# Batch 0's first x made transposed and centred by TensorE, w1 and w2 loaded in other parts, and chunk 0 reordered

## The chip, the core and the metric

The kernel runs on one core of one Trainium2 chip. A core has five engines with an instruction stream each: TensorE (PE in the profile; PEld is its weight load), VectorE (DVE), ScalarE (ACT), GpSimd (POOL) and SyncE (SP). TensorE reads SBUF and writes PSUM, which has eight banks of 512 fp32 columns; the other engines bring results back. The metric is the device time of one execution in microseconds. The time before is 265.41 us, the median of three runs (265.18 to 265.62).

## The reference

Two layers in a row over 8 batches, 8 heads, 576 positions and 64 features a head: a linear attention without a position-by-position matrix, and a normalized two-layer network with a residual.

```
q_s = softmax(q, over features);  k_s = softmax(k, over positions)
kv  = einsum('bhsd,bhse->bhde', k_s, v)          # 64 x 64 per head
x   = einsum('bhsd,bhde->bhse', q_s, kv)         # heads side by side: 512 columns
xn  = (x - mean(x)) / sqrt(var(x) + 1e-6) * g
out = x + relu(xn @ w1) @ w2                     # w1 512 x 2048, w2 2048 x 512
```

All inputs and the output are fp32; the kernel computes its products in bf16. The factor 1/sqrt(var) belongs to a row, so it passes through the relu and both products, and the kernel applies it at the very end.

## The kernel before

The first 512 positions of each batch are one chunk of four tiles of 128 rows (chunks 0 to 7); the last 64 positions of all batches together are chunk 8. A chunk's work is: exp of q and k (ScalarE), the kv products with their division by the sums of exp(k), the transposed exp(q) ("eqT"), x = eqT times kv ("po" in PSUM, evicted to x), xn = 512 x minus the row sum, its transpose "xnT" with 512 columns per tile, then the first product with w1 (PSUM tiles "ph", relu to "hT") and the second with w2 ("pc"). From chunk 2 on, and in chunk 1's second product, a seven-product scheme is used; the change leaves it alone, apart from the last product of the last chunk.

The order of the work on each engine is the order in which the program issues it. `run(main, side)` writes it: `main` is a list of TensorE steps with weights, `side` a list of functions with a position, and a function is issued before the first main step whose summed weight has reached its position. A weight of 1 is a product of 512 moving columns. In chunk 0 the first product fills positions 0 to 64 and the second 64 to 128; in chunk 1 the first product over tiles 0, 1 (32 products of 256 columns, weight 0.5) fills positions 0 to 16, and tiles 2, 3 follow at 16.

What stands around the change:

- `first_batch` (L888) issues the loads and batch 0's start. Loads on SP: q of tiles 0, 1 and k by head pair. Loads on POOL, in order: v, q of tiles 2, 3, w1 in column parts (two of 256, three of 512), w2 in row parts of 512; `load_behind` adds batch 1's and 2's inputs.
- `warm` (L789) issues filler products on TensorE that nothing reads. `z0_mm` (L268) sums exp(k), `kv0_mm` (L284) makes kv of a head pair in PSUM, two pairs to a bank, and evicts them on VectorE.
- `po_half` (L391) makes half of x of tile 0 or 1 and evicts it on ScalarE with its row sum; `sum_halves`, `xn_out` and four transposes with L984 give xnT of tile 0. `exp_qt` is exp of one q tile, `eq_pT` (L877) and `xn_pT` (L880) are four transposes on TensorE and one copy on the engine named in the call; for chunk 0 `xn_pT` multiplies by `g_col` (L866), for the others it is a plain copy (L862 on ScalarE, L864 on VectorE).
- `q0_rest` (L991) is the row sums of exp(q) and x of a later tile of chunk 0, `x_fast` (L380) scales x and makes xn on VectorE, `square_sum` (L365) is ScalarE's sum of squares.
- `mm1_part` (L443) is one step of the first product over part of the tiles, `mm2_stream` (L493) one of the second, `y_out` (L464) the output.
- `mlp_steps` (L745) lists a chunk's main steps; the side lists are at L1044 for chunk 0 and in `second_side` (L818) for chunk 1.
- `last_products` (L574) is the last chunk's second product with its outputs and stores.

PSUM is handed out from two pools: six banks `mm_ps` and two `att_ps`; a tile waits until the bank's earlier user has been read.

Of the kernel before, what the change touches and what calls it, by code (L numbers as in the profile page):

```python
# [20 lines left out]
def kernel(  # L21
# [22 lines left out]
    T = 4  # L44
# [29 lines left out]
    scrap = const.tile([P, 512], BF16)  # L74
    bones = const.tile([P, 2], BF16)
    w1_sb = wts.tile([P, KO1, DH], BF16, tag="w1", name="w1_raw")
    w1g = const.tile([P, KO1, DH], BF16)
    g_col = const.tile([P, KO1], FP32)
    ident_f = const.tile([KO1, KO1], FP32)
# [14 lines left out]
    def load_w2(g4):  # L94
        rows = slice(4 * g4, 4 * g4 + 4)
        nc.gpsimd.dma_start(w2_sb[:, rows, :], w2_src[:, rows, :])
# [182 lines left out]
    def recip_z():  # L279

        kvbox["rz"] = sml.tile([P, NP], FP32, tag="rzk", name="rzk")
        nc.vector.reciprocal(kvbox["rz"], kvbox["z0"][:, 0:NP])

    def kv0_mm(j):  # L284

        if j % 2 == 0:
            kvbox["p0"] = att_ps.tile([P, 2, 256], FP32, tag="a", name="pkv")
        pkv = kvbox["p0"]
        for t in range(T0):
            for ps in halves:  # L290
                nc.tensor.matmul(
                    pkv[ps, j % 2, 0:D], eks[0][ps, j, t], raws["v0"][ps, j, t],
                    start=(t == 0), stop=(t == T0 - 1),
                )
        if j % 2:
            for ps in halves:
                nc.vector.tensor_mul(
                    kv_sb[ps, 0, j - 1 : j + 1, ps], pkv[ps, :, 0:D],
                    kvbox["rz"][ps, j - 1 : j + 1].to_broadcast([64, 2, D]),
                )  # L300

# [44 lines left out]
    def po_mm(c, t, i):  # L346


        if i == 0:
            pool, tag = (mm_ps, "m") if c == 0 and t >= 2 else (att_ps, "a")  # L350
            pobox["p"] = pobox[c, t] = pool.tile([P, DM], FP32, tag=tag, name="po")
# [39 lines left out]
    def po_half(t, half):  # L391

        pool, tag = (mm_ps, "m") if half else (att_ps, "a")
        po = pool.tile([P, DM], FP32, tag=tag, name="po")
        for i in range(2):
            j = 2 * half + i
            nc.tensor.matmul(
                po[:, i * P : i * P + P], eqTs[0][:, t, j, :], kv_sb[:, 0, j, :],
                start=True, stop=True,
            )  # L400
        x, st, _, _ = xs[0]
        nc.scalar.activation(
            x[:, t, DH2 * half : DH2 * half + DH2], po[:, 0:DH2], AF.Copy,
            accum_out=st[:, t, half : half + 1],
        )

    def sum_halves(t):
        _, st, _, mv = xs[0]
        nc.vector.tensor_add(mv[:, t, 0:1], st[:, t, 0:1], st[:, t, 1:2])
# [120 lines left out]
    def prod(n, bank, t, k, first=False, own=False):  # L530
# [13 lines left out]
        nc.tensor.matmul(hbox[bank][:, t], lhsT, rhs, start=first and (own or t == 0) and k == 0,  # L544
# [29 lines left out]
    def last_products(product):  # L574
# [6 lines left out]

        def stt(t, col, src, add=None):
# [17 lines left out]
        def own_bank():  # L600
            bank("d")

        def seed_e():
# [15 lines left out]
        product(4, "d", ts=(1,), own=True, at={  # L619
            15: [lambda: stt(3, 0, hbox["d"][:, 1], part(3, 0)), lambda: store(3, 1, 0)]})  # L620

    def mm2_fast(c):
# [3 lines left out]
        def product(n, name, first=False, at=None, ts=range(2), own=False, cut=None):  # L626
# [4 lines left out]
            for i, (t, k) in enumerate(order):  # L631

                def go(t=t, k=k, i=i):
                    if i == 0 and first:
                        bank(name)
                    prod(n, name, t, k, first or own, own)
# [3 lines left out]
                steps.append((0.5, go))  # L640
# [103 lines left out]

    def mlp_steps(c):  # L745
# [4 lines left out]
        if c == 0:  # L750
            full = range(0)
            parts = ((0, 2, 0, 1), (0, 2, 1, 1), (2, 2, 0, 1), (2, 2, 1, 1), (4, 4, 0, 2), (0, 4, 2, 1),
                     (0, 4, 3, 1), (4, 4, 2, 2), (8, 4, 0, 2), (8, 4, 2, 2), (12, 4, 0, 2), (12, 4, 2, 2))
        else:
            full, parts = range(8, KO2), ((0, 8, 0, 2), (0, 8, 2, 2))
        for m0, mn, t0, tn in parts:
# [5 lines left out]
        if c == 0:  # L762
            return first + [
                (1, lambda t=t, ko=ko: mm2_stream(c, t, ko))
                for n in range(4) for t in range(T) for ko in range(4 * n, 4 * n + 4)
# [52 lines left out]
    def second_side():  # L818

        s = [(p, lambda i=i: quarter_w2(i, 1)) for i, p in enumerate((8.5, 13, 44, 46))]  # L820
        s += [(8.0, lambda: xn_pT(1, 3, nc.vector))]
# [3 lines left out]
        s += [(9 + 2 * j, lambda j=j: cast_v(2, j)) for j in range(2)]  # L825
# [57 lines left out]
    def g_columns():  # L883
        gcp = mm_ps.tile([P, KO1], FP32, tag="m", name="gcp")
        nc.tensor.matmul(gcp, raws["g"], ident_f, start=True, stop=True)
        nc.vector.tensor_scalar_mul(out=g_col, in0=gcp, scalar1=1.0 / DM)

    def first_batch():  # L888
# [30 lines left out]
        nc.vector.memset(ones, 1.0)  # L919
        nc.vector.memset(bones, 0.0)  # L920
# [14 lines left out]
        load_w1(0, 256)  # L935
        load_w1(256, 256)
        for nb in range(1, 4):
            load_w1(512 * nb)
        load_w2(0)
        load_w2(1)  # L940
# [3 lines left out]
        warm(31)  # L944
        for t in range(2):
            exp_qt(0, t)
        exp_k0(0)
        exp_k0(1)
        norm_q(0, 0)
        norm_q(0, 1)  # L950
        eq_pT(0, 0, nc.scalar)
        g_columns()
        exp_k0(2)
        warm(5)
        z0_mm(0)
        z0_mm(1)
        exp_k0(3)
        eq_pT(0, 1, nc.vector)
        z0_mm(2)
        warm(3)  # L960
        z0_mm(3)
        recip_z()
        for j in range(NP):
            kv0_mm(j)
        warm(2)
        po_half(0, 0)
        warm(3)
        po_half(0, 1)
        po_half(1, 0)
        po_half(1, 1)  # L970
# [153 lines left out]
```

## Time and profile before

| | us |
|---|---|
| median of three runs | 265.41 |
| the profiled execution's own time | 265.6 |
| its span, first to last instruction | 263.6 |
| TensorE busy | 257.4 |
| VectorE busy | 217.4 |
| ScalarE busy | 178.8 |
| GpSimd busy | 76.0 |
| first product of chunk 0's first stage (L451) | 15.24 |
| first product of chunk 0's second stage (L497) | 31.84 |
| first product of chunk 1 (L451 on w1g) | 49.21 |

The times in the lower half are starts from the span's first instruction. The profile's views used below are these. The page's first part gives busy time by engine. The waits name the engine and line that waited, what it waited for, the total, how many times and the longest. The chain lists, in order of time, the work that ended last at each moment: start, length, what. A timeline gives start, length, engine, line, operation, written tile <- read tiles, shape and count. Windows give busy time, the share of the DMA engines and what they moved in a stretch. The granted TensorE clock was 0.999 of full speed.

### The profile page before, as it was taken

To read this page: it belongs to the slowest core of one execution; us is meant where nothing else is said; L and a number is where in the kernel's file an instruction comes from. 1 tells how busy PE (TensorE), PEld (TensorE's weight loads), DVE (VectorE), ACT (ScalarE), POOL (GpSimd) and SP (SyncE) were. 2 spreads that over 40 slices of the span, in tenths; PEclk is the share of its full clock that TensorE was granted. 3 is DMA by queue.
4 is the path that set the end of the run, shared out by engine and by line. 5 is a ranking of instruction groups with operands and counts; after the bars stand their busy time and mean duration, and the time that the engine had idled before them with its cause. 6 is when DMAs were issued, how large, how long until landed. Compare 5 with 4: busy or idle time off the path is not lost.

```text
span 263.6 us, 6818 instructions
## 1 busy us (share of the span) xinstructions
PE 257.4 (98%) x2708; PEld 218.1 (83%) x2711; DVE 217.4 (82%) x475; ACT 178.8 (68%) x350; POOL 76.0 (29%) x126
## 2 busy tenths in 40 slices
PE   8989999999999999999999999999999999999993
PEld 5778855775988998899889988998899888888882
DVE  4667797968989997989798979997999889877873
ACT  4467852896966888688868886788678377438400
POOL 8652316203049007600760076008200300030000
PEclk9999999999999999999999999999999999999999
DMA  6999999997986995799879957997804620521014
GB/s 219 256 204 208 338 208 315 271 155 233 207 151 197 325 136 97 197 308 155 93 215 298 139 99 237 297 135 146 256 6 79 161 82 12 71 90 72 0 42 119
DMA packets 69847, 45.00 MB, mean 171 GB/s; under 512 B 41460, under 2 KB 66040, under 8 KB 69816
## 3 DMA queue, kind: packets, MB, share of 16 engines
q1 hardware_dynamic: 48896, 21.76, 39.3%
q0 software_dynamic: 20320, 22.29, 38.9%
q10 hardware_dynamic: 600, 0.53, 0.6%
q8 instruction: 21, 0.34, 0.6%
q14 instruction: 10, 0.08, 0.1%
HBM read 36.70 MB, written 9.44 MB: 175 GB/s over the span
## 4 chain that ended last, share of the span: by engine, by line
PE 92%; DMA 4%; POOL 2%; issue 0%; ACT 0%; DVE 0%; POOLq 0%
PE ba L544 21%; PE bx L688 19%; PE bb L688 9%; PE ph L451 8%; PE bb L544 5%; PE be L544 5%; PE bc L544 5%; PE pc L497 5%; PE bc L688 5%; DMA w_raw<-in_moe_w_ch_dram 4%; PE ph L436 3%; PE po L353 3%; PE pkv L316 2%; PE ptr L860 1%; POOL v L931 1%; PE po L360 1%
## 5 line engine op out<-in xcount | busy, mean ns | idle before, releaser
L544 PEld LDWEIGHTS <-hs 128*128 128x128 bf16 x512 | 49.5, 98 | 5.7
L688 PEld LDWEIGHTS <-w_q 128*128 128x128 bf16 x448 | 43.1, 98 | 5.2 <-issue 0.2
L544 PEld LDWEIGHTS <-hT 128*128 128x128 bf16 x384 | 37.2, 98 | 4.4
L240 POOL TENSOR_TENSOR tq<-xnT 128x256 bf16<-128x256 bf16 x20 | 12.9, 661 | 78.6 <-DMA xnT<-xn 47.2
L688 PEld LDWEIGHTS <-w1g 128*128 128x128 bf16 x336 | 32.2, 98 | 3.9
L544 PE MATMUL ba<-w_q,hs 128*128 128x256 bf16 x256 | 31.7, 273 | 0.0
L688 PE MATMUL bx<-tq,w_q 128*128 128x256 bf16 x224 | 29.0, 273 | 0.0
L561 POOL DMA_DIRECT2D out_dram<-ot x28 | 15.3, 557 | 46.4 <-DVE ot L555 46.4
L367 ACT ACTIVATE scrap<-x,mv 128x512 bf16<-128x512 bf16 x36 | 25.9, 719 | 1.7 <-DVE x L383 1.3
L383 DVE SCALAR_TENSOR_TENSOR x<-po,rq 128x512 bf16<-128x512 f32 x34 | 23.3, 685 | 1.2 <-PE po L353 1.1
L712 ACT COPY bc<-bx 128x512 f32<-128x512 f32 x28 | 15.2, 594 | 13.0 <-PE bx L688 13.0
L719 DVE TENSOR_TENSOR bb<-bx,s 128x512 f32<-128x512 f32 x28 | 18.2, 694 | 6.3 <-ACT s L716 6.3
L730 ACT ACTIVATE hT<-bc 128x512 bf16<-128x512 f32 x28 | 15.3, 595 | 11.9 <-PE bc L688 11.9
L202 DVE TENSOR_REDUCE zq<-eq 128x16 f32<-128x1024 bf16 (+1 forms) x20 | 20.6, 1049 | 2.3 <-ACT eq L193 2.3
L528 DVE TENSOR_TENSOR hs<-hT 128x1024 bf16<-128x1024 bf16 x32 | 20.9, 674 | 0.9 <-ACT hT L730 0.5
L730 ACT ACTIVATE hT<-bb 128x512 bf16<-128x512 f32 x28 | 15.2, 595 | 8.8 <-PE bb L688 8.8
L353 PE MATMUL po<-kv_sb,eqT 128*128 128x128 bf16 x120 | 20.5, 219 | 0.0
L722 DVE TENSOR_TENSOR hT<-bx,s 128x512 bf16<-128x512 f32 x28 | 18.0, 684 | 3.0 <-PE bx L688 3.0
L569 ACT COPY s<-ba 128x512 f32<-128x512 f32 x15 | 8.7, 579 | 12.5 <-PE ba L544 7.8
L544 PE MATMUL ba<-w_sb,hT 128*128 128x256 bf16 x128 | 16.7, 273 | 0.0
L544 PE MATMUL bb<-w_q,hs 128*128 128x256 bf16 x128 | 16.6, 273 | 0.0
L497 PE MATMUL pc<-w_sb,hT 128*128 128x512 bf16 x61 | 15.6, 379 | 0.2
(135 smaller groups left out, 536.9 us busy)
## 6 DMA issues: line engine op xcount, KB each, us to landing
out_dram<-ot POOLq DMA_DIRECT2D x32, 256.0 KB, 5.9
qt<-in_q_dram SPq DMA_DIRECT2D x5, 1024.0 KB, 7.1
kt<-in_k_dram SPq DMA_DIRECT2D x5, 1024.0 KB, 15.0
vt<-in_v_dram POOLq DMA_DIRECT2D x7, 512.0 KB, 14.3
w_sb<-in_moe_w_ch_dram POOLq DMA_DIRECT2D x4, 512.0 KB, 16.1
qt<-in_q_dram POOLq DMA_DIRECT2D x2, 1024.0 KB, 14.8
kt<-in_k_dram POOLq DMA_DIRECT2D x2, 1024.0 KB, 14.3
w_raw<-in_moe_w_ch_dram POOLq DMA_DIRECT2D x3, 512.0 KB, 13.1
```

The source lines that it names most:

```text
L202: nc.vector.reduce_sum(eqs[c][1][:, ts], eqs[c][0][:, ts], axis=AX.X)
L353: nc.tensor.matmul(pobox["p"][:, i * P : i * P + P], eqTs[c][:, t, i, :], kv_sb[:, c, i, :], start=True, stop=True,)
L367: nc.scalar.activation(scrap, x[:, t], AF.Square, bias=mv[:, t, 0:1], scale=-float(DM), accum_out=mv[:, t, 1:2],)
L383: nc.vector.scalar_tensor_tensor(x[:, t].rearrange("p (h d) -> p h d", h=H), in0=pobox[c, t].rearrange("p (h d) -> p h d", h=H), scalar=1. ...
L451: nc.tensor.matmul(ph[:, m % 2, at : at + tn], (w1g if c else w1_sb)[:, ko, m * P : (m + 1) * P], xnTs[c][:, t0 : t0 + tn, ko, :], start=( ...
L497: nc.tensor.matmul(hbox["pc", t], hbox["h"][:, ko, t, :], w2_sb[:, ko, :], start=(ko == 0), stop=(ko == KO2 - 1),)
L528: nc.vector.tensor_tensor(out=dst, in0=x, in1=y, op=op)
L544: nc.tensor.matmul(hbox[bank][:, t], lhsT, rhs, start=first and (own or t == 0) and k == 0, stop=k == KH - 1, skip_group_check=True)
L688: nc.tensor.matmul(dst[:, q], lhsT, rhs, start=first and q == 0 and ko == 0, stop=ko == 1, skip_group_check=True)
L719: nc.vector.tensor_tensor(out=at[g, "b"], in0=at[g, "x"], in1=at[g, "s"], op=ALU.add)
L722: nc.vector.tensor_tensor(out=h_out(g, 1, 1), in0=at[g, "x"], in1=at[g, "s"], op=ALU.add)
L730: nc.scalar.activation(h_out(g, odd, half), at[g, name], AF.Relu)
```

## The change

**Batch 0, tiles 0 and 1.** kv of each head pair gets a PSUM bank of its own. Pairs 0, 2 and 3 are evicted by VectorE, pair 1 by ScalarE, and each eviction also gives the sum of kv's rows (`rs`). ScalarE multiplies a constant matrix of -1/512 by these sums, which gives weights `mean_w` whose product with eqT is minus the row mean of x, on every partition. TensorE then makes x transposed directly: for each of four blocks of 128 features one product with the block's own kv and four with the mean weights, 20 products of 256 columns (tiles 0 and 1 together), in two banks. Blocks 0 and 2 are evicted by ScalarE, 1 and 3 by VectorE, multiplied by g. The old way by `po_half`, `sum_halves`, `xn_out` and transposes goes; x itself, for the residual, is made by eight products, and ScalarE evicts it inside chunk 0 (`x_plain`).

**Loads.** w1's first 512 columns come as two halves of rows, instead of two halves of columns; columns 512 to 1024 as two parts. w2's last rows come as two parts.

**Chunk 0's order.** The first 16 products take tiles 0 and 1 together over the first half of w1's rows and then over the second. The side work of the first stage is set anew. The second stage's last part takes rows 12, 13 and then 14, 15 for tiles 0, 1, and then tiles 2, 3. kv and x of batch 1 move from positions 106 to 119.5 to 111 to 123; the transposes of xn of chunk 1's tile 0 and 1 from 118 and 123 to 121.5 and 126.5, of tile 2 from 128 to position 8 of chunk 1, of tile 3 from position 8 to 14 of chunk 1 and from VectorE to ScalarE.

**The last product** is made in two halves of 128 columns with a bank each, and evicted in two halves.

```diff
+    def kv0_out(j, eng):
+        for ps in halves:
+            dst, src = kv_sb[ps, 0, j, ps], kvbox[j][ps, 0:D]
+            rz, rs = kvbox["rz"][ps, j : j + 1], kvbox["rs"][ps, j : j + 1]
+            if eng is nc.scalar:
+                nc.scalar.activation(dst, src, AF.Copy, scale=rz, accum_out=rs)
+            else:
+                nc.vector.tensor_scalar(
+                    out=dst, in0=src, scalar1=rz, scalar2=0.0, op0=ALU.mult, op1=ALU.add,
+                    accum_out=rs,
                 )
+    def mean0(j):
+        nc.scalar.activation(mean_w[:, j], neg_mean, AF.Copy, scale=kvbox["rs"][:, j : j + 1])
+    def xt_mm(j, i, own, start=False, stop=False):
+        nc.tensor.matmul(
+            kvbox["xt", j % 2][:, j // 2], kv_sb[:, 0, i, :] if own else mean_w[:, i],
+            eqTs[0][:, 0:2, i, :], start=start, stop=stop, skip_group_check=True,
+        )
+    def xt_out(j, eng):
+        src, dst, g = kvbox["xt", j % 2][:, j // 2], xnTs[0][:, 0:2, j, :], g_one[:, j : j + 1]
+        if eng is nc.scalar:
+            nc.scalar.mul(dst, src, g)
+        else:
+            nc.vector.tensor_scalar_mul(out=dst, in0=src, scalar1=g)
...
+    def x_plain(t):
+        x, _, _, mv = xs[0]
+        nc.scalar.activation(x[:, t], pobox[0, t], AF.Copy, accum_out=mv[:, t, 0:1])
...
-        product(4, "d", ts=(1,), own=True, at={
-            15: [lambda: stt(3, 0, hbox["d"][:, 1], part(3, 0)), lambda: store(3, 1, 0)]})
+        product(4, "d", ts=(1,), own=True, half=0, at={15: [lambda: last_half(0)]})
+        product(4, "f", ts=(1,), own=True, half=1, at={15: [lambda: last_half(1), lambda: store(3, 1, 0)]})
...
+    def stream(n):
+        if n < 3:
+            return [(t, ko) for t in range(T) for ko in range(4 * n, 4 * n + 4)]
+        ts = range(2 * n - 6, 2 * n - 4)
+        if n == 4:
+            return [(t, ko) for t in ts for ko in range(12, 16)]
+        return [(t, ko) for k0 in (12, 14) for t in ts for ko in (k0, k0 + 1)]
...
-            parts = ((0, 2, 0, 1), (0, 2, 1, 1), (2, 2, 0, 1), (2, 2, 1, 1), (4, 4, 0, 2), (0, 4, 2, 1),
-                     (0, 4, 3, 1), (4, 4, 2, 2), (8, 4, 0, 2), (8, 4, 2, 2), (12, 4, 0, 2), (12, 4, 2, 2))
+            parts = ((4, 2, 0, 2), (0, 4, 2, 1), (6, 2, 0, 2), (0, 4, 3, 1), (4, 4, 2, 2),
+                     (8, 4, 0, 2), (8, 4, 2, 2), (12, 4, 0, 2), (12, 4, 2, 2))
...
+            first += [
+                (0.5, lambda m=m, ko=2 * kh + ko: mm1_part(c, m, 0, 2, ko))
+                for kh in range(2) for m in range(4) for ko in range(2)
+            ]
...
-        s += [(8.0, lambda: xn_pT(1, 3, nc.vector))]
+        s += [(8, lambda: xn_pT(1, 2, nc.scalar)), (14, lambda: xn_pT(1, 3, nc.scalar))]
...
-        s += [(9 + 2 * j, lambda j=j: cast_v(2, j)) for j in range(2)]
+        s += [(18 + 2 * j, lambda j=j: cast_v(2, j)) for j in range(2)]
...
-        load_w1(0, 256)
-        load_w1(256, 256)
-        for nb in range(1, 4):
+        for kh in range(2):
+            ks = slice(2 * kh, 2 * kh + 2)
+            nc.gpsimd.dma_start(w1_sb[:, ks, 0:512], w1_src[:, ks, 0:512])
+        load_w1(512, 256)
+        load_w1(768, 256)
+        for nb in range(2, 4):
             load_w1(512 * nb)
...
+        warm(16)
+        g_columns()
+        warm(16)
         for t in range(2):
             exp_qt(0, t)
-        exp_k0(0)
-        exp_k0(1)
+        for j in range(NP):
+            exp_k0(j)
         norm_q(0, 0)
         norm_q(0, 1)
+        z0_mm(0)
         eq_pT(0, 0, nc.scalar)
...
         z0_mm(1)
+        warm(3)
         z0_mm(2)
+        warm(2)
         z0_mm(3)
+        eq_pT(0, 1, nc.scalar)
         recip_z()
         for j in range(NP):
+            if j == 3:
+                warm(1)
             kv0_mm(j)
+            kv0_out(j, nc.scalar if j == 1 else nc.vector)
+        for j in range(NP):
+            mean0(j)
...
+        order = (0, 2, 1, 3)
+        for j in range(3):
+            xt_mm(j, j, True, start=(j < 2))
+        for i in range(2):
+            for j in order:
+                xt_mm(j, i, False)
+        xt_mm(3, 3, True)
+        for i in (2, 3):
+            for j in order:
+                xt_mm(j, i, False, stop=(i == 3))
         exp_qt(0, 2)
+        for half, eng in enumerate((nc.scalar, nc.vector)):
+            xt_out(half, eng)
+            xt_out(2 + half, eng)
         exp_qt(0, 3)
+        eq_pT(0, 2, nc.vector)
+        for t in range(2):
+            pobox[0, t] = mm_ps.tile([P, DM], FP32, tag="m", name="po")
...
-        load_w2(2)
+        load_w2(8)
         load_behind(1, (1,))
-        load_w2(3)
+        load_w2(12, 2)
+        load_w2(14, 2)
...
-                (2, lambda: (eq_pT(0, 2, nc.scalar), xn_pT(0, 1, nc.vector), eq_pT(0, 3, nc.scalar))),
-                (2, lambda: (q0_rest(2), x_fast(0, 2))),
-                (6, lambda: q0_rest(3)),
-                (8, lambda: (xn_pT(0, 2, nc.vector), x_fast(0, 3))),
-                (16, lambda: xn_pT(0, 3, nc.vector)),
+                (4, lambda: (eq_pT(0, 3, nc.scalar), x_plain(0), q0_rest(2), x_fast(0, 2))),
+                (8, lambda: (q0_rest(3), xn_pT(0, 2, nc.vector), x_fast(0, 3))),
+                (8.5, lambda: x_plain(1)),
+                (18, lambda: xn_pT(0, 3, nc.vector)),
...
-            + [(106, lambda: (kv_all(1), start_x(1)))]
-            + [(111, lambda: po_x(1, 0)), (113, lambda: po_x(1, 1))]
-            + [(116, lambda: po_x(1, 2)), (118, lambda: xn_pT(1, 0, nc.scalar)), (119, lambda: square_sum(1, 0))]
-            + [(119.5, lambda: po_x(1, 3)), (123, lambda: xn_pT(1, 1, nc.scalar)), (124, lambda: square_sum(1, 1))]
-            + [(128, lambda: xn_pT(1, 2, nc.scalar))]
+            + [(111, lambda: (kv_all(1), start_x(1)))]
+            + [(116, lambda: po_x(1, 0)), (117, lambda: po_x(1, 1))]
+            + [(121.5, lambda: xn_pT(1, 0, nc.scalar)), (122, lambda: square_sum(1, 0))]
+            + [(122.1, lambda: po_x(1, 2)), (123, lambda: po_x(1, 3))]
+            + [(126.5, lambda: xn_pT(1, 1, nc.scalar)), (127, lambda: square_sum(1, 1))]
```

106 lines of the change are left out of this document (38 added, 68 removed).

## The prediction, made before the result was known

> **What bounds the kernel now.** I read the engines' totals first, then what TensorE waited for over the whole span, then the chain that ended last, and last the timelines of the two places that the change rearranges.
>
> ```profile
> PE 257.4 (98%) x2708; PEld 218.1 (83%) x2711; DVE 217.4 (82%) x475; ACT 178.8 (68%) x350; POOL 76.0 (29%) x126
> ```
> ```profile
> PE warm L793 <- DVE bones L920: 1.1, 1, 1.1
> PE ph L451 <- DMA w_raw<-in_moe_w_ch_dram: 0.3, 1, 0.3
> PE zs L872 <- ACT eqT L862: 0.2, 1, 0.2
> PE ptr L983 <- DVE xn L375: 0.2, 1, 0.2
> ```
> TensorE is busy 98% and its listed waits sum to 1.8 us. So a microsecond can be won only in front of its first useful product, or by giving it less to do, and any new wait of TensorE costs its full length. The chain shows where the useful work begins:
>
> ```profile
> 5.78 9.41 DMA w_raw<-in_moe_w_ch_dram
> 15.19 0.06 issue
> 15.24 0.73 PE ph L451 x8
> ...
> 21.44 10.57 PE ph L451 x112
> 32.00 0.21 PE pc L497
> ```
> The first w1 part lands at 15.19, and chunk 0's first products start at 15.24. The second place is the passage from chunk 0 to chunk 1, on TensorE and on ScalarE (start, length, engine, line):
>
> ```profile
> 48.98 0.39 PE L860 MATMUL ptr<-ident,xn 128*128 128x128 bf16 x4
> 49.21 1.91 PE L451 MATMUL ph<-xnT,w1g 128*128 128x256 bf16 x16
> 50.95 0.39 PE L860 MATMUL ptr<-ident,xn 128*128 128x128 bf16 x4
> 51.18 5.40 PE L451 MATMUL ph<-xnT,w1g 128*128 128x256 bf16 x48
> ```
> ```profile
> 48.59 0.72 ACT L367 ACTIVATE scrap<-x,mv 128x512 bf16<-128x512 bf16 x1
> 49.21 0.19 ACT L367 ACTIVATION_READ_ACCUMULATOR scrap<-x,mv 128x1 f32 x1
> 49.41 0.59 ACT L862 COPY xnT<-ptr 128x512 bf16<-128x512 bf16 x1
> 49.89 1.06 ACT L185 ACTIVATE eq<-qt 128x1024 bf16<-128x1024 f32 x1
> 50.85 0.59 ACT L462 ACTIVATE hT<-ph 128x512 bf16<-128x512 f32 x1
> 51.33 1.06 ACT L185 ACTIVATE eq<-qt 128x1024 bf16<-128x1024 f32 x1
> 52.27 1.57 ACT L462 ACTIVATE hT<-ph 128x512 bf16<-128x512 f32 x3
> ```
> ```profile
> 51.38 0.42 DVE L864 COPY xnT<-ptr 128x512 bf16<-128x512 bf16 x1 [0.27 <-PE ptr L860]
> ```
> ScalarE runs without a pause from 49.41, yet TensorE never waits, because tile 3's transposed copy is made by VectorE, ready at 51.80, before tiles 2, 3 are first used (32 products of 0.109 after 49.21, with one set of transposes: 52.92).
>
> **The change, part by part.**
>
> *Start of batch 0.* The memset of the mean weights and the copy to g_one (about 0.17 and 0.155, rows L917 and L886) fall where VectorE idles until 5.75. TensorE, with 32 fillers and the gain's transposition ahead of z, reaches z at about 7.7 and has 1.65 of work up to the last z, which can start at 9.84: cover 0.5. ScalarE's last exp of k still ends at 9.79, since it waits for its load. Then ScalarE copies both eqT tiles (0.59 each, the second after its transposes): 11.2. TensorE does the last z at 9.84, transposes at 10.13, and the four kv products (72 in 1.11 now, 0.28 a pair) until 11.71. The kv evictions are a shape the trace lacks, 64x64 with a sum: on VectorE between 0.155 (L886, 4 columns) and 0.288 (L297, 128 columns); I take 0.22 plus 0.08 for reading the sum, 0.45 a pair after overlap, so pairs 0, 2, 3 are out at 11.35, 11.9, 12.4, and pair 1 on ScalarE (0.2 to 0.38, rows L418 and L402, plus 0.19) at 11.94. The four mean weights need a column as scale. A 512-column ScalarE operation with such an operand takes 0.72 (L367), without 0.59 (L862), so 0.13 more; L402's 256 columns take 0.38, so 128 columns take about 0.27, with the operand 0.39, started 0.29 apart: 12.23 to 13.11. [...]
>
> TensorE's 20 new products of 256 columns take 20 x 0.109 = 2.18: with the waits for kv and means they run 11.8 to 14.3. Evictions: ScalarE two of 0.38 + 0.11 from 14.13, VectorE two of 0.42 (L984's) from 14.35, done at 15.0 and 15.1; the first of each, which is all that the first products need, at 14.77. Beside these TensorE makes eqT 2's transposes and po of tiles 0, 1 (0.22 + 8 x 0.055): 14.82. Bounds of this point: 14.6 and 15.5, by both ends of the unseen rows.
>
> *w1 in other parts.* The first part has the same 256 KB, in lines twice as long. In windows of the trace the short lines moved 200 GB/s (12 to 15 us) and the long 208 (18 to 21), which brings the part in 0.05 to 0.1 earlier. In the packet records 15 of its 16 shares landed by 14.14 and the last at 15.19, behind a 16 KB instruction packet that took 0.95 from 13.12. TensorE's instructions number about as many up to there, so I expect the packet again and the part at 15.1 (bounds 14.1 and 15.3). The start then goes from 15.24 to 15.15: gain 0.09, with bounds of +0.4 and -0.3.
>
> POOL issues one DMA more (w2's last rows as two). Its queue issues the ninth when the first has landed, and so on, so q of batch 1 goes out when the first w1 part has landed. All that stands ahead of w2's last rows is the same bytes; they land at 43.4 now, and TensorE needs them at 44.42 now, 43.5 then for rows 12, 13 and 44.3 for 14, 15. No wait, with 0.9 spare.
>
> *Chunk 0's first stage.* From 15.24 to the first L497 at 31.84 it takes 16.60. New: 32 products of 128 columns at 0.0556 and 112 of 256 at 0.1092 = 14.01 (now 64 and 96, 14.04); three sets of transposes, 0.67 (now five, 1.11); zs and po of tiles 2, 3, 0.67: 15.35. Waits, from latencies in this trace: from the zs of tile 2 to its xn takes 1.75 (16.88 to 18.63), and only 1.54 of work stands between: 0.21. From the last transpose to a finished L866 takes 1.0 (21.22 to 22.21): before tile 2's products 0.93 of work stands in between (0.07), before tile 3's only four products, 0.49 (0.51). Sum 15.35 + 0.79 = 16.14: gain 0.46. The plain x copies on ScalarE (0.59 + 0.19 each) lie beside this.
>
> *Chunk 0's end.* kv and x of batch 1 move five products later or so; the same products, with the same 0.14 wait between kv and po. VectorE keeps its run of x, xn and output steps; its casts of v (2 x 0.42) go behind TensorE's first 36 products of chunk 1, where nothing reads them until L316 at 58.5. No store and no load changes its place in POOL's or SP's order. Call T the time at which chunk 1's products begin, less tile 2's transposes (48.98 now, about 48.4 then).
>
> *Tiles 2, 3 of chunk 1.* Their transposes now stand after 16 and 28 of chunk 1's products, and **both copies are on ScalarE**, in its order: exp of q, relu, exp, relu, copy 2, relu, copy 3. Tile 1's transposes now end one product before T, so its copy starts at T and its square ends with the sum read at T + 1.29 (steps as at 48.11, 48.59, 49.41). From there by the rows' start-to-start steps: exp 0.96, relu 0.48, exp 0.96, relu 0.48, copy 0.48, relu 0.48, copy 0.59: T + 5.72. TensorE has done 32 products and two sets of transposes at 32 x 0.1092 + 2 x 0.22 = T + 3.94, and the next product reads tiles 2 and 3. It waits **1.8 us**, with everything behind it in its order (bounds 1.4 and 2.1, from 0.1 to 0.3 either way in ScalarE's head start). Behind the copy on ScalarE stand relu and exp of k, whose users are later than the wait. The row already shows the copy at 0.59 on ScalarE and 0.42 on VectorE. [...]
>
> *The end.* The last product is cut into halves, each with its own bank: 16 x 0.056 for 8 x 0.109, 0.02 more; the last VectorE step shrinks from 0.48 to about 0.35. ScalarE's last store issue ends at 260.80, 0.3 behind SP's, and had waited for its own earlier issue, so I take 0.08 of gain (0 to 0.13).
>
> Sum: -0.09 - 0.46 + 1.80 - 0.08 = **+1.17**. The profiled execution took 265.6 (span 263.6), 0.2 over the median of 265.41; 265.41 + 1.17 = **266.6**.
>
> **The rivals.** *The copies are not late (faster).* Only ScalarE's queue at T decides. If tile 3's copy ended by T + 4.57, 1.17 sooner than I sum, the wait would be under the 0.63 won, and with no wait the time is 264.8. For it: ScalarE sits idle 4.5 us just before (46.58 in its timeline), so a little less work ahead of T empties its queue. Against: from T on every term is a row of this trace. *The new start is slow.* If the sums and means cost their upper ends, first products start at 15.5: +1.5, 266.9; this lies within the forecast. *w2's last rows are late.* They are issued by a queue that waits for landings; if the second half came at 45.3, a second wait of 1.0 follows: 267.6. For: it is one more DMA behind k's landing at 34.58; against: the queue holds 7 us of bytes then. *The gain in front is larger.* With no instruction packet in the way the start is 14.85: +0.87, 266.3, also within the forecast.
>
> **How the numbers follow.** Copies late, as summed with its bounds (265.9 to 267.3): 0.72. Copies in time: 0.15. w2 late: 0.06. In between, with a wait of about 0.6 that cancels the gain: 0.07. A measurement of this kernel tells about 0.2%, 0.5 us, from no change. So slower 0.78, same 0.07, faster 0.15. The range reaches down to the top of the faster case and over the one in between, 264.9, and up to 267.4.
>
> **What would show it.** Right: in the trace of the changed kernel TensorE waits at L451 on ScalarE's xnT some 5 us after chunk 1 begins, about 1.8 long, with relus and exps back to back on ScalarE; first L497 near 31.3; 20 products of the transposed x between 11.8 and 14.4; first L451 product at 15.1 with a DMA wait. Wrong: no wait in chunk 1, or a first L497 before 30.7 or after 31.9, or waits for w_sb near 44.

## The result, and the profile after

The changed kernel takes **267.28 us** (266.73 to 268.78, 6 runs) against 265.37 us (265.18 to 265.62, 6 runs) for the kernel before: 1.0078 times as long, 95% interval 1.005 to 1.0106. It is slower by 1.9 us, where 1.2 was forecast. Times are medians here and below, and ratios are of means; one execution of the kernel before, at 1512.5 us beside the ninth and tenth experiments, is left out of the ratios. The execution that was profiled, 266.75 us with a span of 264.5, is one of its two fastest, and it lies 1.15 over the profiled 265.6 of before. So the sum of the prediction, +1.17, holds for this execution, and not for the middle of the runs. Both facts have to be explained.

The page's totals:

```profile
PE 256.8 (97%) x2700; PEld 217.5 (82%) x2700; DVE 216.3 (82%) x479; ACT 181.8 (69%) x357; POOL 77.2 (29%) x128
```
TensorE has 0.6 us less work in a span that is 0.9 longer. Its waits say where the rest went (engine, line, tile, what it waited for: total, times, longest):

```profile
PE warm L832 <- DVE ones L959: 1.1, 1, 1.1
PE ph L464 <- DVE zq L205: 0.9, 1, 0.9
PE ph L464 <- ACT xnT L901: 0.5, 1, 0.5
PE z L277 <- ACT ek L269: 0.4, 1, 0.4
PE ph L464 <- DVE xnT L905: 0.3, 1, 0.3
```
The wait for w1's load (0.3 before) is gone, and three waits of `ph` at L464 are new, two of them at the passage to chunk 1. TensorE's timeline, first at the start of chunk 0 and then at the passage to chunk 1, gives their places:

```profile
14.75 1.05 PE L464 MATMUL ph<-xnT,w_raw 128*128 128x256 bf16 x8
...
21.34 9.79 PE L464 MATMUL ph<-xnT,w_raw 128*128 128x128 bf16 x96 [0.34 <-DVE xnT L905]
30.96 4.05 PE L510 MATMUL pc<-w_sb,hT 128*128 128x512 bf16 x18
...
47.74 0.39 PE L899 MATMUL ptr<-ident,xn 128*128 128x128 bf16 x4
47.96 0.38 PE L510 MATMUL pc<-w_sb,hT 128*128 128x512 bf16 x1
48.80 1.91 PE L464 MATMUL ph<-xnT,w1g 128*128 128x256 bf16 x16 [0.46 <-ACT xnT L901]
50.54 0.39 PE L899 MATMUL ptr<-ident,xn 128*128 128x128 bf16 x4
50.76 1.47 PE L464 MATMUL ph<-xnT,w1g 128*128 128x256 bf16 x12
52.07 0.39 PE L899 MATMUL ptr<-ident,xn 128*128 128x128 bf16 x4
52.30 0.60 PE L464 MATMUL ph<-xnT,w1g 128*128 128x256 bf16 x4
53.82 3.65 PE L464 MATMUL ph<-xnT,w1g 128*128 128x256 bf16 x32 [0.93 <-DVE zq L205]
```
The first second-stage product (L510, L497 before) starts at 30.96 instead of 31.84: in this execution the front wins 0.88. At the passage the listed waits are 0.46 and 0.93. Counted in whole gaps, one product of 512 columns after 47.96 takes 0.22 and the next could start at 48.18, but starts at 48.80: 0.62. Four products after 52.30 take 0.44, so 52.74, but the next starts at 53.82: 1.08. Together **1.70**. ScalarE's timeline shows what the second is for, whatever the wait's name says:

```profile
48.16 0.59 ACT L901 COPY xnT<-ptr 128x512 bf16<-128x512 bf16 x1 [0.45 <-PE ptr L899]
48.64 0.72 ACT L395 ACTIVATE scrap<-x,mv 128x512 bf16<-128x512 bf16 x1
49.27 0.19 ACT L395 ACTIVATION_READ_ACCUMULATOR scrap<-x,mv 128x1 f32 x1
49.36 1.04 ACT L188 ACTIVATE eq<-qt 128x1024 bf16<-128x1024 f32 x1
50.31 0.58 ACT L475 ACTIVATE hT<-ph 128x512 bf16<-128x512 f32 x1
50.78 1.05 ACT L188 ACTIVATE eq<-qt 128x1024 bf16<-128x1024 f32 x1
51.73 0.59 ACT L475 ACTIVATE hT<-ph 128x512 bf16<-128x512 f32 x1
52.21 0.59 ACT L901 COPY xnT<-ptr 128x512 bf16<-128x512 bf16 x1
52.67 0.62 ACT L475 ACTIVATE hT<-ph 128x512 bf16<-128x512 f32 x1
53.16 0.61 ACT L901 COPY xnT<-ptr 128x512 bf16<-128x512 bf16 x1
```
Tile 1's copy ends at 48.75, 0.05 before the first product of chunk 1; tile 3's at 53.77, 0.05 before the product at 53.82. The releaser named by the wait, VectorE's sum of q, is only the last semaphore event near it. From there on nothing changes: the first `ba` product of chunk 1 comes at 65.70 instead of 64.80 (+0.90 = 1.70 - 0.88 and 0.08 of small pieces), and the span ends 0.9 later. The time around the span grew too, from 2.0 to 2.25 us.

### The profile page after: what moved, and what is told of

The parts are those of the page before. It is cut to its first block, busy times and chain, and to the rows that moved or that the text cites. A ratio compares the mean times of both kernels' runs of the same rounds, so it can differ in the third digit from the quotient of the medians.

```text
span 264.5 us, 6811 instructions
## 1 busy us (share of the span) xinstructions
PE 256.8 (97%) x2700; PEld 217.5 (82%) x2700; DVE 216.3 (82%) x479; ACT 181.8 (69%) x357; POOL 77.2 (29%) x128
## 5 line engine op out<-in xcount | busy, mean ns | idle before, releaser
L737 ACT COPY bc<-bx 128x512 f32<-128x512 f32 x28 | 15.2, 593 | 13.0 <-PE bx L713 13.0
L755 ACT ACTIVATE hT<-bb 128x512 bf16<-128x512 f32 x28 | 15.2, 595 | 8.8 <-PE bb L713 8.8
L510 PE MATMUL pc<-w_sb,hT 128*128 128x512 bf16 x64 | 15.6, 379 | 0.0
```

The lines of the kernel that those rows point to most:

```text
L510: nc.tensor.matmul(hbox["pc", t], hbox["h"][:, ko, t, :], w2_sb[:, ko, :], start=(ko == 0), stop=(ko == KO2 - 1),)
L755: nc.scalar.activation(h_out(g, odd, half), at[g, name], AF.Relu)
```

## The experiments

The theory (A): the loss is ScalarE's queue at the passage, as predicted. The rivals: something in front that varies from one execution to the next, such as the landing of w1's parts (B); pauses that let TensorE's clock fall behind the passage (C); and, after the first runs, a fall of the clock within the new front (D) or the landing of k's last part alone (E). C does not hold in the profile above: the 32 products from 53.82 on end where the next begin, at 57.31, which is 0.109 each as before the change, at a granted clock of 1.00. The kernel before was run beside each of the four groups of experiments (1 to 4, 5 to 8, 9 and 10, 11, in the order told here); its medians were 265.66, 265.57, 265.61 and 265.46. Lines of the changed kernel are unchanged up to one or two in the experiments.

**The changed kernel once more**

> The changed kernel itself, once more, to see whether its time splits into two groups (266.7 to 266.9 and 267.6 to 268.8 so far) while the kernel before does not. Theory A (the loss is TensorE's two waits for ScalarE's copies of xnT at the passage to chunk 1, 0.62 and 1.08 us, less 0.9 gained in front): about 1.4 over the kernel before, 266.7, in every run, and the two waits in the profile again. Rival B (something in front that varies, such as the landing of w1's parts): other times in other runs, up to 3 over, with a later first L464 or a DMA wait at L464 before 20 us. Rival C (the pauses of TensorE let its clock fall): products of 256 columns at more than 0.109 us apart behind 54 us.

267.51 us (266.88 to 267.96, 5 runs), ratio 1.0071 (1.0059 to 1.0083). The waits at the passage are the same, but the front is another one:

```profile
PE ph L464 <- ACT xnT L901: 1.4, 2, 0.9
```
Here the clock reached full speed at 6.75 us instead of 3.71, the first product of L464 came at 15.29 instead of 14.75 and the first L510 at 31.63 instead of 30.96. That is a gain of 0.2 over the kernel before, not 0.9, with the same instructions. The loss of 1.85 us stands, where theory A with a gain of 0.9 in front gave 1.4, so the first profile shows one of the earliest fronts and not a typical one.

**Tile 3's copy back to VectorE**

```diff
-        s += [(8, lambda: xn_pT(1, 2, nc.scalar)), (14, lambda: xn_pT(1, 3, nc.scalar))]
+        s += [(8, lambda: xn_pT(1, 2, nc.scalar)), (8, lambda: xn_pT(1, 3, nc.vector))]
```


> The changed kernel with one line back: the transposes of chunk 1's tile 3 at position 8 and its copy on VectorE. Theory A: ScalarE is then done with tile 2's copy at about 52.8, when TensorE gets there (52.74); the second wait shrinks from 1.08 to 0.1, the first (0.6, tile 1's copy) stays; the time is 1.0 less than the changed kernel's. Rivals B and C: the time stays within 0.3 of the changed kernel's, or the wait only moves to another line.

266.54 us (265.6 to 267.84, 9 runs), ratio 1.0038 (1.0017 to 1.0059): 0.97 less than the run beside it. The second wait is gone, the first stays (`ACT xnT L901: 0.5`). That is theory A for 1.0 of the loss. The profiled execution, 267.71, brought something else; TensorE's timeline and then the windows of 3.41 us in it (busy time of each engine, granted clock, DMA share):

```profile
8.77 0.45 PE L277 MATMUL z<-ones,ek 64*64 64x1 bf16 x18 [0.25 <-ACT ek L269]
9.15 0.39 PE L832 MATMUL warm<-junk 128*128 128x256 bf16 x2
10.44 0.45 PE L277 MATMUL z<-ones,ek 64*64 64x1 bf16 x18 [0.90 <-ACT ek L269]
10.81 0.61 PE L899 MATMUL ptr<-ident,eq 128*128 128x128 bf16 x4
11.35 1.65 PE L294 MATMUL pkv<-v,ek 64*64 64x64 bf16 x54
...
16.87 1.04 PE L464 MATMUL ph<-xnT,w_raw 128*128 128x256 bf16 x8
```
```profile
3.92:7.33 3.41, 3.14 (x42) 2.37 (x41) 1.95 (x6) 2.15 (x4) 3.41 (x6) 1.00 1.06 360
7.33:10.75 3.42, 2.27 (x63) 1.49 (x63) 1.35 (x3) 1.99 (x4) 1.85 (x3) 1.00 1.18 244
10.75:14.16 3.41, 3.41 (x89) 2.79 (x84) 1.51 (x10) 2.25 (x9) 2.41 (x4) 0.50 1.16 229
```
The last part of k landed at 9.68 (8.61 in the first profile), TensorE waited 0.90 for its exp, and then the clock fell to half for 3.41 us, in the middle of the products that the front is made of: 54 products of kv took 1.65 (1.04 in the fourth experiment's profile). First product at 16.87. This is theory D, and it was not in the prediction. Of the 2.1 us by which that is later than in the first profile, 1.07 had come by the start of the last z (10.44, and 9.37 there), which k's landing had set, and 1.05 came behind it, at half clock.

**The kernel before with nothing but the new order of chunk 0's end and chunk 1's start**

```diff
-            + [(106, lambda: (kv_all(1), start_x(1)))]
-            + [(111, lambda: po_x(1, 0)), (113, lambda: po_x(1, 1))]
-            + [(116, lambda: po_x(1, 2)), (118, lambda: xn_pT(1, 0, nc.scalar)), (119, lambda: square_sum(1, 0))]
-            + [(119.5, lambda: po_x(1, 3)), (123, lambda: xn_pT(1, 1, nc.scalar)), (124, lambda: square_sum(1, 1))]
-            + [(128, lambda: xn_pT(1, 2, nc.scalar))]
+            + [(111, lambda: (kv_all(1), start_x(1)))]
+            + [(116, lambda: po_x(1, 0)), (117, lambda: po_x(1, 1))]
+            + [(121.5, lambda: xn_pT(1, 0, nc.scalar)), (122, lambda: square_sum(1, 0))]
+            + [(122.1, lambda: po_x(1, 2)), (123, lambda: po_x(1, 3))]
+            + [(126.5, lambda: xn_pT(1, 1, nc.scalar)), (127, lambda: square_sum(1, 1))]
...
-        s += [(8.0, lambda: xn_pT(1, 3, nc.vector))]
+        s += [(8, lambda: xn_pT(1, 2, nc.scalar)), (14, lambda: xn_pT(1, 3, nc.scalar))]
```


> The kernel before with only the new order from position 106 on (kv and x of batch 1, the transposes of xn of chunk 1, the casts of v). Theory A: both waits appear without any of the new front, 0.6 and 1.1, and the time is 1.7 over the kernel before, 267.1. Rival: the new order costs only beside the new front, so within 0.4 of the kernel before.

267.19 us (267.06 to 267.6, 5 runs), ratio 1.0065 (1.0053 to 1.0077): +1.53, with the old front and its range of 0.5. TensorE's timeline has the same two waits at the same two places:

```profile
49.91 1.91 PE L451 MATMUL ph<-xnT,w1g 128*128 128x256 bf16 x16 [0.46 <-ACT xnT L862]
...
54.93 2.23 PE L451 MATMUL ph<-xnT,w1g 128*128 128x256 bf16 x19 [0.92 <-ACT xnT L862]
```
So the new order alone costs 1.5, without any of the new front, and A needs no rival for that. For the rest B is not out: the new front was to win 0.6 against these 1.5, and the changed kernel loses 1.9.

**Both waits taken away, the new front kept (below: the repaired kernel).** Tile 1's transposes go 2.5 positions earlier and its square sum into chunk 1, and tiles 2 and 3 are transposed at 8, the second for VectorE.

```diff
-            + [(126.5, lambda: xn_pT(1, 1, nc.scalar)), (127, lambda: square_sum(1, 1))]
+            + [(124, lambda: xn_pT(1, 1, nc.scalar))]
...
-        s += [(8, lambda: xn_pT(1, 2, nc.scalar)), (14, lambda: xn_pT(1, 3, nc.scalar))]
+        s += [(8, lambda: xn_pT(1, 2, nc.scalar)), (8, lambda: xn_pT(1, 3, nc.vector))]
+        s += [(16.5, lambda: square_sum(1, 1))]
```


> The changed kernel with ScalarE's queue shortened: tile 1's transposes at 124 in place of 126.5, its sum of squares behind chunk 1's first 33 products, tile 3's copy on VectorE. Theory A: neither wait is left (0.1 at most), so the front's gain of 0.9 shows: 0.6 to 0.8 under the kernel before, 264.6 to 264.8. Rivals B and C: still slower than the kernel before.

265.35 us (264.63 to 267.26, 12 runs), ratio 1.0005 (0.9985 to 1.0025). No wait for ScalarE is left at the passage:

```profile
PE warm L832 <- DVE ones L960: 1.1, 1, 1.1
PE ph L464 <- DVE xnT L906: 0.3, 1, 0.3
PE pc L510 <- issue: 0.2, 1, 0.2
```
It is 2.16 faster than the changed kernel beside it. Yet it is level with the kernel before, where a front that always gave 0.9 would have won that less 0.2 around the span. Its runs show why: eight of twelve lie between 264.63 and 265.56, one at 266.51 with a full clock, and three at 266.5 to 267.3 with a mean clock of 0.991 or 0.992, which is what 3.41 us at half speed, as in the second experiment's profile, make of 265 us (0.9936), and a little more for the last two microseconds, where TensorE has nothing left to do and the clock was at half again in that profile (from 263.34 of 265.5 us).

**More and fewer products that keep TensorE busy between the z's.** Eleven fillers of 256 columns instead of five, and none:

```diff
         z0_mm(1)
-        warm(3)
+        warm(5)
         z0_mm(2)
-        warm(2)
+        warm(6)
         z0_mm(3)
```


> The version with ScalarE's queue shortened, with 11 fillers in place of 5 between the z products of batch 0. Theory D (the new front leaves TensorE short of work between 7 and 11 us, since the sums of exp(k) have one moving column each; where a window of that stretch is too empty the clock falls to half for 3.4 us, and the front grows by about 1.5): no profile and no run with the clock fallen, so the upper group (266.5 to 267.3 without these fillers) is gone, the median falls to 265.0, and the best stays within 0.4 of 264.63. Rival E (the spread is the landing of k's last part alone, 8.5 to 9.7 us): the upper group stays.

265.89 us (265.31 to 266.99, 12 runs), ratio 1.0008 (0.9993 to 1.0024).

> The same version with no filler between the z products. Theory D: the clock falls in most executions, mean clock 0.99 in them, and the median rises by 1 to 2, to 266.4 or more. Rival E: fillers do not matter, the median stays within 0.3 of 265.35.

265.96 us (264.95 to 266.36, 10 runs), ratio 1.0007 (0.999 to 1.0024). With none, four of ten runs have a clock of 0.991 to 0.993, at 265.95 to 266.31; with eleven, no run of twelve is below 0.996, but the best time is 265.31 instead of 264.95: the fillers make the start later by what they save (first product at 15.16 and 14.53 in the two profiles). So the fall went with fewer fillers for TensorE between 7 and 11 us: they are the only difference, and 4 of 10 against 0 of 12 would come by chance about once in 35 times. (With five fillers it was 3 of 12 in the fourth experiment and 0 of 12 in the tenth.) Neither median came as expected, 265.0 and 266.4 or more. The fall is not all of the spread: with eleven fillers the times still reach over 1.7 us at a clock of 0.996 to 1.0, so a landing such as k's (E) is not out for the rest.

**w1's first columns in column halves, as before, under the new front**

```diff
-        for kh in range(2):
-            ks = slice(2 * kh, 2 * kh + 2)
-            nc.gpsimd.dma_start(w1_sb[:, ks, 0:512], w1_src[:, ks, 0:512])
-        load_w1(512, 256)
-        load_w1(768, 256)
-        for nb in range(2, 4):
+        load_w1(0, 256)
+        load_w1(256, 256)
+        for nb in range(1, 4):
             load_w1(512 * nb)
```


> The version with ScalarE's queue shortened, with w1's first 512 columns in two halves of columns again, and 512 to 1024 in one part. The first eight products then need both of the first parts, of which the second landed at 15.9 in the kernel before, instead of 14.7. By the prediction's step (the start is set by w1's landing) the first L464 goes from 14.8 to about 16.0 and the time up by 0.9 to 1.2. Rival (the start is set by x, and the parts are worth nothing): within 0.3.

265.91 us (265.36 to 267.2, 10 runs), ratio 1.001 (0.9991 to 1.0028); its best run is 0.73 over the best of the kernel with row halves, from another group of runs, but the intervals do not tell the two apart. The profiled execution has two waits in front, and only the second is w1's:

```profile
PE ptr L900 <- ACT eq L196: 0.9, 1, 0.9
PE ph L464 <- DMA w_raw<-in_moe_w_ch_dram: 0.4, 1, 0.4
```
The second wait is only 0.4 long because the first had already cost 0.9. w1's second part landed at 16.45, so the second four of the first eight products would have started at 16.49 without the first wait too; with row halves they follow the first four without a gap, from 15.28 in the fourth experiment's profile (14.84 + 0.44). By landing the parts are worth 1.2 in that execution, at the upper end of what was expected; the medians, 0.6 apart, are from two groups. The first wait is taken up with the last two runs below. The time around the span was 2.05 here, as before the change, and 2.2 to 2.35 in the ten profiles with row halves. As this edit also takes one DMA away (columns 512 to 1024 come in one part again), it does not tell which of the two counts.

**The changed kernel with the old order of the end** (the third experiment's edit the other way round)

> The changed kernel with the old order from position 106 on. Theory A: no wait of TensorE for ScalarE at chunk 1. But kv of batch 1 then reaches TensorE at 40.9, before ScalarE has its exp of the last k rows (42.05, as they land at 41.5), so TensorE waits there for about 0.8. Net 0.9 under the changed kernel, 266.4. Rival: the front's gain is real and nothing holds it, 264.9.

266.19 us (265.98 to 267.57, 12 runs), ratio 1.0022 (1.0007 to 1.0038): 1.1 to 1.3 less than the changed kernel, and 0.6 over the kernel before, as expected in size, though the wait that is listed has another reason. The waits:

```profile
PE pkv L345 <- DVE vm L137: 1.0, 1, 1.0
```
Batch 1's kv, at its old place, waits for VectorE's casts of v, which run from 41.20 to 42.09, behind a row of VectorE's w1 sums. The expected reason stands right behind it: ScalarE's exp of the last k rows ends at 42.57, 0.05 before the product that reads it, so without the casts TensorE would have waited there about as long. So the front being earlier makes work at position 106 come before what it reads, and a later place for it was needed; the changed order gave that and made ScalarE late instead.

**Ten fillers, fewer before the z's, and tile 3's transposes one position earlier; and beside it the fourth experiment's kernel again**

> The version with ScalarE's queue shortened, with the same work for the clock at less cost: 10 fillers in place of 16 behind the gain's transposition, 5 and 5 in place of 3 and 2 between the z products, and the transposes of chunk 0's tile 3 at 17 in place of 18. Theory D: TensorE reaches z by 6.9 even where the clock rises late, the clock falls in few runs, chunk 0's wait for tile 3 goes from 0.5 to 0.3; median 264.9, 0.6 to 0.8 under the kernel before. Rival E (the spread comes from when k's last part lands): as many runs over 266 as without it, median within 0.2 of that version's.

265.39 us (264.85 to 266.33, 11 runs), ratio 0.9991 (0.998 to 1.0002). No run is below a clock of 0.996, but the expected median of 264.9 did not come. Its profiled execution is its slowest, 266.33, and the front is not what is late in it: the first product comes at 15.08, and the first `ba` product of chunk 1 at 64.22, as in the fifth experiment's profile (64.23, in an execution of 265.31). It loses 1.04 behind that (in whole gaps), at two waits in the first product of chunk 2:

```profile
PE bb L713 <- POOL tq L243: 0.5, 1, 0.5
PE bx L713 <- ACT s L741: 0.2, 1, 0.2
```
GpSimd makes `tq` from the transposed xn, which a DMA brings. Here it waited for that DMA until 76.92 (75.68 in the fifth experiment's profile), and `bb` started at 78.27 instead of 77.61. So what this execution lost owes nothing to the front.

> The version with ScalarE's queue shortened, on the same chip beside the one with spread fillers. Theory D: some 3 of 12 runs with a mean clock of 0.992 or less and 1.5 to 2 over the others; median 265.3, best 264.6, 0.2 to 0.4 under the kernel before.

265.22 us (264.93 to 266.34, 12 runs), ratio 0.9991 (0.9978 to 1.0003). Some three falls of the clock were expected here, and none came: no run fell below 0.996. Its profiled execution was one of the two longest, 266.11 at full clock, and shows one more source of spread, in the front. ScalarE's timeline, then TensorE's, of this profile:

```profile
14.40 0.63 ACT L196 ACTIVATE eq<-qt 128x512 bf16<-128x512 f32 x1 [1.36 <-DMA qt<-in_q_dram]
15.06 0.84 ACT L327 ACTIVATE xnT<-xt,g_one 128x256 bf16<-128x256 f32 x2
```
```profile
15.09 0.40 PE L900 MATMUL ptr<-ident,eq 128*128 128x128 bf16 x4 [0.84 <-ACT eq L196]
15.32 0.61 PE L1035 MATMUL po<-kv_sb,eqT 128*128 128x128 bf16 x8
15.77 1.04 PE L464 MATMUL ph<-xnT,w_raw 128*128 128x256 bf16 x8
```
The exp of q's tile 2 stands on ScalarE ahead of its evictions of the transposed x, and on TensorE that tile's transposes stand ahead of the first product. q's second half landed at 14.38; in the first profile of the same kernel at 12.80, and the first product came at 14.84. In the packet records 15 of the 16 shares had landed at 12.76 here: the last one stood behind a 16 KB instruction packet that began at 12.08 and took 1.2 (matched by their times, as the records do not name the DMA engine). In the other profile the packet (11.80) is matched in the same way with a share of w1's first part instead, for which nothing waited. The column-halves profile above has the same (15 shares at 12.52, the last at 14.12).

**q's landing taken off the path.** VectorE evicts blocks 0 and 1, ScalarE 2 and 3, and tile 2's transposes go behind the second product.

```diff
-        for half, eng in enumerate((nc.scalar, nc.vector)):
-            xt_out(half, eng)
-            xt_out(2 + half, eng)
+        for j in range(4):
+            xt_out(j, nc.vector if j < 2 else nc.scalar)
         exp_qt(0, 3)
-        eq_pT(0, 2, nc.vector)
...
+                (1, lambda: eq_pT(0, 2, nc.vector)),
```


> The kernel of the run ahead with one more change in front: nothing that chunk 0's first products read stands behind the exp of q's tile 2 any more. VectorE evicts blocks 0 and 1 of the transposed x (a bank of their own) and ScalarE blocks 2 and 3, the first eight products go by k block, and tile 2's transposes move from ahead of the first product to behind the second. In the second profile of that kernel q's second half landed at 14.38 instead of 12.80, ScalarE waited for it (1.36), TensorE 0.84 behind it, and the first product came at 15.77 instead of 14.84, at full clock. Theory: that landing makes the slow runs at full clock. Then the first product comes at 14.6 to 14.8 wherever q lands up to 14.4, the runs above 266 at full clock disappear, and the median is 264.9 to 265.1, faster than before by 0.4 to 0.6. Rival: the spread comes from the time around the span, from k's landing or from the clock; then runs above 266 stay and the median is 265.2 to 265.4, as for the run ahead. A second rival: the shorter cover in front of tiles 2 and 3 gives the gain back as a wait for tile 3's copy, 0.35 now, then 0.6 or more, and the median is 265.3 to 265.6.

265.45 us (265.03 to 267.08, 12 runs), ratio 1.0001 (0.9984 to 1.0018). The median of 264.9 to 265.1 did not come. The ten runs with a full clock lie at 265.03 to 265.58, none above 266, which fits the theory (three of the 21 such runs of the kernel without this edit were), but twelve runs are too few to prove it, and the kernel before has such runs too: 8 of its 94 beside the experiments lie above 266 at full clock, up to 267.51. Two runs fell to a clock of 0.992 and took 266.7 and 267.1. And the step from the first `xt` product to the first L510 took 19.26 in this profile against 19.18: what the shorter way to the first product gave went into transposes moved behind it.

## Why the prediction was right and wrong

**Right: the passage to chunk 1.** The term was +1.80, bounds 1.4 to 2.1; it is 1.70 in the first profile, and the third experiment shows it alone at 1.53, the fourth shows it gone. ScalarE's order came out as listed (copy, square, exp, relu, exp, relu, copy, relu, copy), and from the start of tile 1's copy at 48.16 to the end of tile 3's at 53.77 it took 5.61, with 5.72 predicted. One piece was overlooked: the first product of chunk 1 already reads tile 1, so 0.62 of the wait comes there. Since TensorE then starts later by as much, the wait for tile 3's copy is shorter by as much, and the total is the same.

**Right: chunk 0's first stage.** 14.75 to 30.96 is 16.21, with 16.14 predicted and 16.60 before. The waits summed there, 0.79, came as gaps of 0.28 before tile 2's transposes (17.38 to 17.66) and 0.51 before tile 3's products (20.83 to 21.34, of which 0.34 is listed). **Right: w2's last rows**, with no wait. **Near: the end.** VectorE's last step took 0.35 as predicted; from the first `ba` to VectorE's end it is 0.04 less, and 0.08 was predicted.

**Luck: the sum in the profiled execution.** The start was 0.40 better than its term, the passage 0.1, the first stage and the end 0.1 worse together, and the time around the span, for which the sum had no term, 0.2 worse. These nearly cancel.

**Wrong: the start of batch 0**, the term of -0.09 with bounds of +0.4 and -0.3. In the prediction the start was "15.24 to 15.15", fixed by w1's landing as in the one profiled execution. The packet behind which w1's last share landed came a microsecond earlier, 12.0 instead of 13.1, and w1's first part landed at 14.71; and the steps ahead (20 products from 11.66 to 14.03, forecast 11.8 to 14.3) were on time or better. That made 14.75, outside the bounds on the good side. But the step's real fault is that it gave one number. In the kernel before, TensorE runs fillers until w1 is there, so whatever varies ahead of 15.2 is hidden, and no fall of the clock shows: none of 95 executions of it beside the experiments had a mean clock below 0.995. The new front has no such slack, and its first product came at 14.53 to 16.87 in eleven profiles, by four things: when the clock rises (3.71 or 6.75 us: 0.54 between the two profiles of the changed kernel), when k's last part lands (8.61 or 9.68: 1.07), whether the clock falls back (1.05 in the one profile that has it), and whether q's second half lands late, behind the instruction packet (0.93). The range of a term should have been taken from what its cover was, and what varies behind that cover.

Of the clock itself the profiles show this much: it rose to full speed at 3.71 us in the first profile, at 6.75 in the second and at 7.01 in the kernel before, and in the one profile with a fall it was at half from 10.75 to 14.16. In the 3.42 us before that fall TensorE was busy for 2.27, with 54 of its 63 products of one column. What sets the time of a rise or a fall is not shown.

**Also wrong: 0.2 us around the span**, which the sum put at nothing. It is in every execution: the time less the span is 2.2 to 2.4 in all that have the row halves, and 1.9 to 2.1 in the kernel before. No view of the profiles shows what it consists of.

The sum by these terms: the middle of the runs lies 0.7 over the forecast, and 0.2 of that is the time around the span. The forecast had 0.63 in favour of the change. In the repaired kernel that came at the median of the spans: 263.1 and 263.0 in the fourth and tenth experiments, against 263.7 and 263.6 for the kernel before beside them. Its median times show only 0.3 to 0.4, as the time around the span takes the rest. For the changed kernel that makes -0.35 + 1.70 = +1.35; it measured +1.9 and +1.85. The difference of 0.5 is in the span, and not in the passage, whose gaps are 1.69 in the second profile of the changed kernel (1.70 in the first). It lies within what the fronts of single executions differ by (in that second profile the front won 0.2 instead of 0.9), but no run here divides it further.

**The rivals.** Copies in time, given 0.15: no. w2 late, 0.06: no. A slow new start, with first products at 15.5, came in three of the eleven profiles (15.51, 15.77 and 16.87), but not through the sums and means, whose last weight was done at 12.99 in the first profile (13.11 forecast). A larger gain in front was seen in the profiled execution, where the packet came earlier but was not out of the way, and not in the one after it.

What stays open: the 0.2 around the span, which goes with w1's row halves in all profiles and is not explained by them; what the remaining 0.5 of the changed kernel's loss is; and the spread at full clock, 1.7 us with eleven fillers, of which q's landing explains one profile (the tenth experiment's) and a late load in chunk 2 another (the ninth's).

None of these kernels is faster than the kernel before by more than the measurement tells.

## What to carry to other kernels

When a wait is taken out of a front, ask what it had been hiding: slack ahead of a late load also hides a late landing, a late clock and a fall of the clock, and without it each of them showed here, by 0.54 to 1.07 us, so the gain came as a spread. When a copy or an order moves to another engine, write out that engine's queue from the moment at which the reader needs the result; here this sum was right to 0.1 us. A kernel that is ahead of its old schedule by a microsecond meets waits that the old one just missed (batch 1's kv at its old place waited 1.0), so what is placed by position has to be placed again.

## What the runs showed of the hardware

- The clock fell to half for 3.41 us (10.75 to 14.16, second experiment). In the 3.42 us before, TensorE was busy 66% by the profile, with 54 of its 63 products of one column. No fall came in the two profiles where it was busy 2.51 and 2.57 of 3.41 us, 74 and 75% (11.42 to 14.83 in the profile with column halves, 12.50 to 15.91 in the tenth experiment's). Over the runs with the new front a mean clock below 0.995 came in 4 of 10 with no fillers, 10 of 78 with five and 0 of 23 with ten or eleven.
- In three profiles one of a load's 16 shares landed 1.05 to 1.62 us after the other 15, and the load was complete only then: w1's first part at 15.19 behind 14.14 before the change and at 14.71 behind 13.58 in the first profile, q's second half at 14.38 behind 12.76 in the tenth experiment's. In each a 16 KB packet of the instruction queue, 0.95 to 1.2 us long, had begun at 13.12, 12.02 and 12.08. That it held up the share is the author's reading of these times. TensorE had made 205 products by then before the change, and 195 in the first profile.
- GpSimd issued its ninth load 0.28 to 0.29 us after its first, v's, had landed: at 10.11 behind 9.82 before the change, and at 9.60 behind 9.32 in the first profile. There its thirteenth, q of batch 1, went out at 14.99, 0.28 behind its fifth, w1's first part (14.71).
- An eviction of 64x64 from PSUM with a sum took 0.28 + 0.08 us on VectorE and 0.31 + 0.19 on ScalarE in the first profile; the prediction had taken 0.22 + 0.08 and about 0.29 + 0.19.
